# Decode block, forward and backward: Wo products of the second batch held back to row 47, and the first store tile lent by the loads for one gV only

## The chip, the cores and the metric

The kernel runs on one core of one Trainium2 chip. The metric is device time in microseconds (us), the median of several runs. The profile is of one execution.

## The reference, cut to what matters

One decode step of a pre-layernorm block with a KV cache, and the gradients of all its inputs but the constant `B_x`. There are 2 batches, 32 heads, a cache of 4096 positions and heads of 128; the model width is 640, the MLP's 1728; everything is bfloat16.

```python
q = layernorm(x) @ wq                          # [2, 32, 1, 128]
p = softmax(q @ k_cache^T * Dh**-0.5)          # per (batch, head), over 4096 positions
o = p @ v_cache
h = x + o @ wo
out = h + relu(layernorm(h) @ w1) @ w2
# and the vjp of out with grad_out:
# gV = p outer go, gK = (p * (go.V - go.o)) outer q * Dh**-0.5      [2, 32, 4096, 128] each
# go = wo @ gh, and the gradients of x, wq, wo, w1, w2
```

One (batch, head) has a K tile and a V tile of 128 x 4096 values, 1 MB each. All 64 are read, V of most heads a second time, and 64 gV and 64 gK tiles of 1 MB each are written: 211 MB read and 149 MB written in all.

## The kernel before, in words

**Rows.** The program is a hand-made plan of rows. Row i runs three steps of the forward pass for three neighbouring (batch, head) pairs: scores of pair i (K transposed by TensorE, `t_ps` into `t_sb`, then `s_ps`), the softmax and the products of K with the weights for pair i-1 (`pk`, two halves on VectorE), and the products with V for pair i-2 (`m_ps`, `u_ps`). A row has eight stages, k = 0 to 7, each ended by a `yield` in `p1_iter`. Rows 0 to 31 are the heads of batch 0 and rows 32 to 63 those of batch 1. Every 1 MB load is named here by kind and pair: K 46 is the K tile of pair 46, needed in row 46; V 43 is the V tile of pair 43, needed in row 45; W is a V tile read again for the backward pass.

**Between the stages.** After a stage of a row the loop takes, in this order: steps of the backward generator `p2_iter` (rows 41, 43, 45 and so on each begin a backward head j = 0, 1, 2; a head's steps run at k = 1 (two), 3, 4 and 6 of its own row and at k = 1, 4 and 6 of the next), at k = 5 `a_heads`, then `pump`, which issues the loads for which a tile is free, then a share of the background generators. One of these, `middle_gen(0)`, runs from row 34 on: it is the MLP of batch 0 and the gradient of its attention output, in the order layernorm, w1 products, gradient, `gh1c`, spread of `gh1c` over the partitions (`bcb_ps`), and then `go_group` for a few heads at a time (`goc`, `pr_ps`, `gom`, `d_ps`, `negdot`). Backward head j can only begin when its go is done.

**Wo products.** `a_heads(i)` does one of two things at most: `o_group`, which scales the outputs of four heads and casts them (`OU`, `OFc`, two small VectorE operations), or `a_group`, 20 TensorE products of them with Wo into `a_ps`, added to `asum` by VectorE. `a_ps` lies in the PSUM bank `mid` (bank 7), as do `pr_ps`, `d_ps` and others; the role `bc` (`bcb_ps`) takes bank 2 and bank 7 in turn in rows 34 to 40. For batch 1 the first `o_group` becomes due at row 38, and one more every four rows; `a_group` follows in the next row.

**Tiles.** Thirteen 1 MB tiles in SBUF have one of four owners, above all the loads (`ld`) and the stores (`g`). `take(tag)` hands out the tile that was given back first to that owner; `give(t, to)` gives it back, to another owner if `to` says so. A tile taken again waits, in the engine that first writes it, for all that read it before: a load waits in SyncE's queue, a gradient tile in VectorE's order waits for the landing of the store that read it. The V tiles of the last six heads of batch 0 (turns j = 0 to 5) stay in SBUF and are the W tiles of those heads, so from row 33 to row 40 seven tiles rotate among the loads. At row 40 the K tile that comes free goes to the stores (line 566). W of head 0 goes to them at row 41, W of head 2 at row 45; from then on the stores own three.

**Backward head, j < 2 (`early`).** gV is made in two VectorE halves (line 844 from 896 and 908) while W is still being transposed, and stored by GpSimd's queue (line 909); then the last score products, `gsp`, and gK in two halves (lines 938 and 940), stored at line 941. For j >= 2 gV is made after W's transposes. Loads are issued by SyncE (line 445), stores of gK and gV by GpSimd. The lines that give tiles back:

```python
        give(c["W"], "g" if j < H and j != 1 and owned["g"] < 3 else None)     # 915
        if early:
            give(gV)                                                          # 918
            yield
```

Of the kernel before, what the change touches and what calls it, by code (L numbers as in the profile page):

```python
# [15 lines left out]
def kernel(  # L16
# [23 lines left out]
    _, H, Sk, Dh = A_k_cache.shape  # L40
# [64 lines left out]
    def give(t, to=None):  # L105
        tag, k, _ = home_of.pop(id(t))
        to = to or goes_to(tag)
        owned[tag] -= 1
        owned[to] += 1
        free[to] += 1  # L110
        homes[to].append(k)
        given_at[k] = step[0]
# [736 lines left out]
    def last_dp(j, c):  # L849

        b, h = turns[j]
        pair_matvec(c["dp"], c.pop("T3"), 3, gom[:, h, b, :, :])
# [10 lines left out]
    def p2_iter(j, busy, act=0, own_gK=False, early=False):  # L863

        c = S2[j] if j < NP1 else None
        p = S2.get(j - 1)
        if p is not None:
            bp, hp = turns[j - 1]
            last_dp(j - 1, p)
            gsp = score_grad(j - 1, p)  # L870
        if c is not None:
            b, h = turns[j]
            go = gom[:, h, b, :, :]

            bank = pst([128, 512], FP32, "sps", "dp_ps")
            for k, col in enumerate((goc, qsc)):
                nc.tensor.matmul(bank[:, 128 + k * 128:256 + k * 128],  # L877
                                 lhsT=col[:, h, b:b + 1].to_broadcast([128, 128]), rhs=ident_bf[:],
                                 start=True, stop=True)
            c["dp"] = bank[:, 0:NSC]  # L880
            rb = mats.tile([128, 256], BF16, tag="rb", bufs=3, name="rb")
            nc.scalar.activation(out=rb[:], in_=bank[:, 128:384], func=ACT.Copy, scale=rt[:, b, h:h + 1])  # L882
            pp = small.tile([128, NSC, 2], BF16, tag="pp", bufs=2, name="pp")
            nc.gpsimd.tensor_copy(out=pp[:], in_=P_bf[:, b * H + h, :, None].to_broadcast([128, NSC, 2]))
            c.update(rb=rb, pp=pp)
            if act:
                pa = small.tile([128, 8], FP32, tag="pa", bufs=2, name="pa")
                nc.gpsimd.tensor_copy(out=pa[:], in_=P_bf[:, b * H + h, NSC - act:NSC])
            c["T0"] = pair_transpose(c["W"], 0, busy=busy)
        if p is not None:  # L890
            gK = take("g", [128, NSC, 128], "gK")
            outer_half(gK, p["rb"][:, 128:256], gsp, 0)
        yield
        if early:
            gV = take("g", [128, NSC, 128], "gV")
            outer_half(gV, c["rb"][:, 0:128], c["pp"], 0)
        if p is not None:
            outer_half(gK, p["rb"][:, 128:256], gsp, 1)
            nc.gpsimd.dma_start(out=natural(out_2, bp, hp), in_=gK[:])  # L899
            give(gK)  # L900
            del S2[j - 1]
        yield
        if c is None:
            return
        c["T1"] = pair_transpose(c["W"], 1, busy=busy)
        pair_matvec(c["dp"], c.pop("T0"), 0, go)
        if early:
            outer_half(gV, c["rb"][:, 0:128], c["pp"], 1)
            nc.gpsimd.dma_start(out=natural(out_3, b, h), in_=gV[:])
        yield  # L910
        c["T2"] = pair_transpose(c["W"], 2, busy=busy)
        pair_matvec(c["dp"], c.pop("T1"), 1, go)
        yield
        c["T3"] = pair_transpose(c["W"], 3, busy=busy)
        give(c["W"], "g" if j < H and j != 1 and owned["g"] < 3 else None)
        pair_matvec(c["dp"], c.pop("T2"), 2, go)
        if early:
            give(gV)
            yield
            last_dp(j, c)  # L920
            gsp = score_grad(j, c)
        else:
            gV = take("g", [128, NSC, 128], "gV")
            outer_half(gV, c["rb"][:, 0:128], c["pp"], 0)
            yield
            if own_gK:
                last_dp(j, c)
            outer_half(gV, c["rb"][:, 0:128], c["pp"], 1, act)
            for k in range(act):
                nc.scalar.activation(out=gV[:, NSC - act + k, :], in_=c["rb"][:, 0:128], func=ACT.Copy, scale=pa[:, k:k + 1])  # L930
            nc.gpsimd.dma_start(out=natural(out_3, b, h), in_=gV[:])  # L931
            give(gV)
            if own_gK:
                gsp = score_grad(j, c)
            yield
        if own_gK:
            gK = take("g", [128, NSC, 128], "gK")
            outer_half(gK, c["rb"][:, 128:256], gsp, 0)
            yield
            outer_half(gK, c["rb"][:, 128:256], gsp, 1)  # L940
            nc.gpsimd.dma_start(out=natural(out_2, b, h), in_=gK[:])
            give(gK)
            del S2[j]
            yield
# [217 lines left out]
    i = j = 0  # L1162
# [58 lines left out]
    for n, (i, j) in enumerate(plan):  # L1221
        all_go = all(("go", B - 1, h) in done for h in range(H))
        if i is None and plan[n - 1][0] is not None:
            pkp.release()
            big1 = tc.alloc_tile_pool(name="big1", bufs=1)
            for _ in range(2):
                more_home("ld", big1)
            share(ld=KEPT[1] + 4, g=5)
        if all_go and not late[0]:
            wop.release()  # L1230
            big3 = tc.alloc_tile_pool(name="big3", bufs=1, side="right")
            for tag in ("ld", "g", "g", "q", "q", "q"):
                more_home(tag, big3)
        late[0] = all_go
        more = int(late[0])
        if fin is not None and not bg2 and not bg3:
            share(ld=8 + 3 * more, g=7 + 3 * more)
        elif fin is not None and j >= H + KEPT[1] - 1:
            share(ld=5 + more, g=6 + 2 * more, f=3, q=2 + 3 * more)
        if j is not None:  # L1240
            while g2 is not None:
                p2_step()
            if j < NP1:
                bg_until(("go", *turns[j]))
            g2 = p2_iter(j, 0, 8 if i is None and j <= H else 0, i is not None and plan[n + 1][1] is None, j < EARLY)
        if i is None and ("w1", 1) in done and fin is None:
            wts.release()
            fin = tc.alloc_tile_pool(name="fin", bufs=1)
            big2 = tc.alloc_tile_pool(name="big2", bufs=1)
            more_home("f", big2)  # L1250
            banks.update(sps=[2, 3], o=[4, 5, 6])
            bg2.append(("fin", fin_gen(fin)))
            bg3.append(("gx", gx_gen(fin)))
        if i == 12:
            bg.append(("ga", ga_gen()))
        if i == H + 2:
            banks["bc"].insert(0, banks["sps"].pop(0))
        elif i == P2_AT:
            banks["bc"].remove(7)
            banks["sps"].insert(0, banks["bc"][0])  # L1260
            banks["bc"] = [7]
        rate = RATES[0 if i is not None and i <= H + 1 else 1 if j is None and i < P2_AT else
                     2 if i is not None else 3 if j <= H else 4]
        if i is None:
            spread[0] = 2
            at_k[0] = 1
            k = 0
            while g2 is not None:
                p2_step()
                pump()  # L1270
                slot[0] = int(k in ((1, 3, 5) if j <= H else (1, 4)))
                k += 1
                bg_step(0, rate)
                bg_step(1, RATE2 * (0.4 if spreading[0] else 1.0))
                bg_step(2, RATE3)
            continue
        at = MIXED if j is not None else REST
        for k, _ in enumerate(p1_iter(i, i < H + 1, 0)):
            for _ in range(at.get(k, 0)):
                if g2 is not None:  # L1280
                    p2_step()
            if k == 5:
                a_heads(i)
            pump()

            spread[0] = 1 if i < P2_AT else 2
            at_k[0] = k
            if i >= P2_AT:
                slot[0] = int(k == 6 or (k == 1 and j is not None))
            elif i > H + 1:  # L1290
                slot[0] = {1: 2, 3: 1, 4: 1, 6: 1}.get(k, 0)
            else:
                slot[0] = int(k in (1, 6))
            bg_step(0, rate)
            bg_step(1, 0.0)
        if i is not None and i in (H + 1, NP1 + 1):
            bg.append((f"m{i // H - 1}", middle_gen(i // H - 1)))
# [41 lines left out]
```

## Time and profile before

| what | value |
|---|---|
| runs shown | 889.36 us median of 3 (888.87 to 893.23) |
| the profiled execution | 888.85 us, span 886.6 us |
| busy: PE, PE weight loads, DVE, ACT, POOL | 83%, 70%, 77%, 56%, 23% |
| DMA | 361.85 MB, mean 408 GB/s |
| mean granted TensorE clock | 0.774 |
| loads of K and V: issue to landing, median | 17.3 and 18.4 us |
| stores of gV and gK: issue to landing, median | 13.6 and 14.1 us |

The page gives busy time by engine (PE is TensorE, DVE VectorE, ACT ScalarE, POOL GpSimd, SP SyncE), then the span in 40 equal slices. The mean rate of 408 GB/s stands beside slices of 410 to 427; the slices under that show where the DMA engines were not filled. Rows 35 to 52 of the plan, which the change touches, lie at about 210 to 345 us. A window's line gives its bounds, its length, the busy time and the number of instructions of each engine, the granted TensorE clock, the busy share of the DMA engines and the rate.

### The profile page before, as it was taken

How to read it: one execution, taken by the hardware profiler on the slowest of the kernel's cores; microseconds unless marked ns; L12 is line 12 of the kernel's file. 1: busy time of each engine (PE TensorE's matmuls, PEld its weight loads, DVE VectorE, ACT ScalarE, POOL GpSimd, SP SyncE). 2: the span in 40 equal slices, each digit the busy share in tenths (PEclk: the TensorE clock that was granted, in tenths of full speed). 3: DMA queues.
4: the chain of work that ended last, by engine and by line, in shares of the span. 5: the costliest groups of instructions: out<-in, count | busy, mean ns of one | idle time of the engine just before them, and what ended most of it. 6: DMA issues, size and time to landing. Idle time of an engine off the chain costs nothing.

```text
span 886.6 us, 24742 instructions
## 1 busy us (share of the span) xinstructions
PE 738.5 (83%) x10145; PEld 616.7 (70%) x10145; DVE 681.9 (77%) x1284; ACT 498.6 (56%) x1292; POOL 201.9 (23%) x358
## 2 busy tenths in 40 slices
PE   4999899899999999788868876878877898556794
PEld 4887788788888888778758766666656666345463
DVE  2666788877878897696778978878887789579964
ACT  1444343346777665455536768777656766435663
POOL 1344434443312010010012322222221111011111
PEclk9999999999999999898985555555566757556555
DMA  9999999999979999999999999999999999999997
GB/s 378 423 421 414 417 408 416 426 423 412 351 278 410 419 423 424 425 425 425 417 415 394 418 420 422 418 420 417 419 414 397 423 426 419 427 425 424 404 376 314
DMA packets 56289, 361.85 MB, mean 408 GB/s; under 512 B 5680, under 2 KB 11760, under 8 KB 15472
## 3 DMA queue, kind: packets, MB, share of 16 engines
q1 hardware_dynamic: 34520, 211.13, 57.8%
q0 software_dynamic: 18432, 134.23, 36.5%
q10 hardware_dynamic: 3224, 14.92, 4.1%
q8 instruction: 80, 1.31, 0.5%
q14 instruction: 33, 0.27, 0.1%
HBM read 211.11 MB, written 149.13 MB: 406 GB/s over the span
## 4 chain that ended last, share of the span: by engine, by line
PE 32%; DMA 31%; DVE 20%; ACT 8%; issue 7%; SPq 1%; POOL 0%; ACTq 0%; POOLq 0%; DVEq 0%
DMA Vt<-in_A_v_cache_dram 13%; PE t_ps L424 13%; PE m_ps L460 8%; DMA out_dram<-gK 7%; DVE gK L844 5%; DMA wqs<-in_A_wq_dram 5%; DVE gV L844 4%; DVE gxj L677 4%; ACT gV L930 3%; DMA out_dram<-gV 3%; PE s_ps L437 3%; DVE pk L470 3%; PE u_ps L498 2%; ACT t_sb L429 2%; PE dp_ps L437 2%
## 5 line engine op out<-in xcount | busy, mean ns | idle before, releaser
L429 ACT COPY t_sb<-t_ps 128x512 f32<-128x512 f32 x479 | 273.1, 587 | 204.5 <-PE t_ps L424 200.1
L437 PEld LDWEIGHTS <-t_sb 128*128 128x128 bf16 x4096 | 178.6, 102 | 60.8 <-ACT t_sb L429 33.6
L424 PE MATMUL t_ps<-ident_f,Wt 128*128 128x128 f32 x832 | 199.6, 391 | 0.8 <-ACT t_sb L429 0.8
L460 PE MATMUL m_ps<-pk,Vt 128*128 128x129 bf16 x2048 | 171.3, 222 | 17.1 <-DMA Vt<-in_A_v_cache_dram 16.2
L470 DVE TENSOR_TENSOR pk<-Kt,ep 128x2048 bf16<-128x2048 bf16 (+1 forms) x128 | 152.7, 1193 | 34.7 <-ACT ep L524 19.6
L844 DVE TENSOR_TENSOR gK<-rb,gsp 128x2048 bf16<-128x2048 bf16 x128 | 153.3, 1225 | 11.8 <-DMA out_dram<-gV 10.2
L424 PEld LDWEIGHTS t_ps<-ident_f,Wt 128*128 128x128 f32 x832 | 138.7, 202 | 29.9 <-issue 23.0
L460 PEld LDWEIGHTS <-Vt 128*128 128x128 bf16 x2048 | 125.1, 99 | 48.2 <-issue 28.7
L424 PE MATMUL t_ps<-ident_f,Kt 128*128 128x128 f32 x1024 | 154.3, 284 | 4.9 <-DMA Kt<-in_A_k_cache_dram 4.2
L844 DVE TENSOR_TENSOR gV<-rb,pp 128x2048 bf16<-128x2048 bf16 (+1 forms) x128 | 142.7, 1139 | 12.2 <-DMA out_dram<-gK 7.8
L486 POOL COPY pk<-ep 128x16 bf16<-128x16 bf16 x80 | 84.1, 1053 | 157.5 <-ACT ep L524 81.8
L424 PEld LDWEIGHTS t_ps<-ident_f,Kt 128*128 128x128 f32 x1024 | 112.8, 144 | 8.1 <-issue 3.3
L437 PE MATMUL dp_ps<-gom,t_sb 128*128 128x2 bf16 x2048 | 96.1, 168 | 22.5 <-ACT t_sb L429 22.3
L931 POOL DMA_DIRECT2D out_dram<-gV x62 | 33.0, 532 | 313.3 <-DVE gsp L858 116.9
L437 PE MATMUL s_ps<-qm,t_sb 128*128 128x2 bf16 x2048 | 87.3, 164 | 1.9 <-DVE t_sb L427 1.5
L986 ACT CAST ot<-o_ps 128x512 bf16<-128x512 f32 (+3 forms) x152 | 67.6, 491 | 8.0 <-DMA out_dram<-ot 3.9
L588 ACT CAST MT<-m_ps 128x128 bf16<-128x128 f32 x64 | 17.0, 266 | 91.6 <-PE m_ps L460 91.4
L899 POOL DMA_DIRECT2D out_dram<-gK x53 | 28.2, 532 | 138.5 <-DVE gK L844 104.7
L882 ACT ACTIVATE rb<-dp_ps,rt 128x256 bf16<-128x256 f32 x64 | 30.3, 473 | 46.1 <-PE dp_ps L877 45.5
L677 DVE CUSTOM_DVE_ANT_0 hbc<-wo_t,hbc 128x640 bf16<-128x640 bf16 x64 | 52.9, 826 | 0.3
L677 DVE CUSTOM_DVE_ANT_0 gxj<-wqs,gqr 128x1024 bf16<-128x1024 bf16 x40 | 48.7, 1219 | 1.2 <-DMA wqs<-in_A_wq_dram 0.9
L858 DVE SCALAR_TENSOR_TENSOR gsp<-dp_ps,negdot,P_bf 128x64 bf16<-128x64 f32 x64 | 17.9, 279 | 39.6 <-PE dp_ps L437 39.6
(205 smaller groups left out, 786.0 us busy)
## 6 DMA issues: line engine op xcount, KB each, us to landing
Kt<-in_A_k_cache_dram SPq DMA_DIRECT2D x64, 1024.0 KB, 17.3
Vt<-in_A_v_cache_dram SPq DMA_DIRECT2D x64, 1024.0 KB, 18.4
out_dram<-gV POOLq DMA_DIRECT2D x64, 1024.0 KB, 13.6
out_dram<-gK POOLq DMA_DIRECT2D x64, 1024.0 KB, 14.1
Wt<-in_A_v_cache_dram SPq DMA_DIRECT2D x52, 1024.0 KB, 11.2
wq_t<-in_A_wq_dram SPq DMA_DIRECT2D x5, 1024.0 KB, 10.0
wo_t<-in_A_wo_dram SPq DMA_DIRECT2D x4, 1280.0 KB, 18.4
wqs<-in_A_wq_dram SPq DMA_DIRECT2D x5, 1024.0 KB, 17.8
```

The lines of the kernel that those rows point to most:

```text
L424: nc.tensor.transpose(t_ps[:, j, :], natf[:, 2 * cc:2 * cc + 2, :].rearrange("p c k -> p (c k)"), ident_f[:])
L429: nc.scalar.copy(out=t_sb[:], in_=t_ps[:])
L437: nc.tensor.matmul(dst[:, sc:sc + 2], lhsT=v[:, j, :, par], rhs=vecs[:, par, :], start=(par == 0), stop=(par == 1))
L460: nc.tensor.matmul(r["m"][:, 0:129], lhsT=r["V"][:, sc, :], rhs=r["pk"][sc // HALF][:, sc % HALF, 0:129], start=(sc == 0), stop=(sc == NSC ...
L470: nc.vector.tensor_tensor(out=p["pk"][k][:, 0:n, 0:128].rearrange("p s (a two) -> p s a two", two=2), in0=p["K"][:, sl, :].rearrange("p s ...
L486: nc.gpsimd.tensor_copy(out=col, in_=e)
L677: nc.vector.tensor_tensor_reduce(out=junk[0:kc, 0:width], in0=in0, in1=in1, scale=1.0, scalar=0.0, op0=ALU.mult, op1=ALU.add, accum_out=acc)
L844: nc.vector.tensor_tensor(out=pairs_view(dst[:, sl, :]), in0=row.rearrange("p (a two) -> p a two", two=2)[:, None, :, :].to_broadcast([128 ...
L882: nc.scalar.activation(out=rb[:], in_=bank[:, 128:384], func=ACT.Copy, scale=rt[:, b, h:h + 1])
L899: nc.gpsimd.dma_start(out=natural(out_2, bp, hp), in_=gK[:])
L931: nc.gpsimd.dma_start(out=natural(out_3, b, h), in_=gV[:])
L986: nc.scalar.copy(out=ot[0:P, k, n0:n0 + nn], in_=o_ps[0:P, 0:nn])
```

## The change

```diff
         c["T3"] = pair_transpose(c["W"], 3, busy=busy)
-        give(c["W"], "g" if j < H and j != 1 and owned["g"] < 3 else None)
+        give(c["W"], "g" if j < H and owned["g"] < 3 + (j == 0) else None)
         pair_matvec(c["dp"], c.pop("T2"), 2, go)
         if early:
-            give(gV)
             yield
+            give(gV, "ld" if j == 0 else None)
             last_dp(j, c)
             gsp = score_grad(j, c)
...
-            if k == 5:
+            if k == 5 and not H + 2 < i < P2_AT + 6:
                 a_heads(i)
```

H is 32 and P2_AT is 41, so `a_heads` is not called in rows 35 to 46. The groups that were due there follow from row 47 on, one call a row. The tile of head 0's gV goes back to the loads, one stage of the plan after W's transposes (row 42, k = 1), instead of to the stores. W of head 1 goes to the stores; before, it went to the loads. From row 45 on the loads own ten tiles and the stores three, as before.

## The prediction

> **What bounds the kernel now.** I read the page's slices first, then windows of 2 us over the one hole in them, then the chain of waits there, and last the timelines of VectorE (DVE), GpSimd (POOL) and SyncE (SP).
>
> The page's slices, each 22.2 us:
>
> ```profile
> PEclk9999999999999999898985555555566757556555
> DMA  9999999999979999999999999999999999999997
> GB/s 378 423 421 414 417 408 416 426 423 412 351 278 410 419 423 424 425 425 425 417 415 394 418 420 422 418 420 417 419 414 397 423 426 419 427 425 424 404 376 314
> ```
>
> DMA sits at 410 to 427 GB/s nearly everywhere. The hole is 351 and 278, from 222 to 266 us. Outside it, time is bytes over rate, so what counts is how many microseconds of transfer a change adds or takes away. Windows over the hole's end (columns: PE, PE loads, DVE, ACT, POOL busy, PE clock, DMA share, GB/s):
>
> ```profile
> 258.00:260.00 2.00, 1.79 (x32) 1.48 (x33) 2.00 (x4) 1.71 (x6) 0.00 (x0) 1.00 0.39 160
> 260.00:262.00 2.00, 2.00 (x41) 1.60 (x34) 2.00 (x4) 0.64 (x2) 0.00 (x0) 1.00 0.03 8
> 262.00:264.00 2.00, 1.95 (x35) 1.70 (x32) 1.79 (x4) 1.11 (x5) 0.69 (x1) 1.00 0.41 172
> 264.00:266.00 2.00, 2.00 (x36) 1.98 (x36) 0.87 (x3) 1.89 (x8) 0.29 (x1) 1.00 1.08 319
> 266.00:268.00 2.00, 2.00 (x39) 1.41 (x37) 2.00 (x3) 1.48 (x4) 0.98 (x1) 1.00 0.89 340
> 268.00:270.00 2.00, 2.00 (x33) 1.86 (x30) 2.00 (x4) 1.95 (x9) 0.89 (x2) 1.00 1.01 426
> ```
>
> At 260 to 262 nothing is in flight: the loads wait for tiles, the first store has not begun, and PE and DVE are full. Row 41 begins near 255, row 42 near 263, row 43 near 269.5. Whatever shortens rows 38 to 41 brings the filled DMA forward. The chain of waits at row 39:
>
> ```profile
> 247.31 1.13 DVE pk L470
> 248.44 0.08 DVE asum L613
> 248.53 0.04 issue
> 248.57 0.44 PE bcb_ps L645 x5
> 249.01 0.88 PE t_ps L424 x8
> 249.89 0.07 PE s_ps L515
> ```
>
> PE waits for asum, because bcb_ps takes the PSUM bank that a_ps held, and asum stands in DVE's order behind a pk half.
>
> **Part one, Wo products.** Rows 35 to 46 no longer call a_heads. Gone from the hole: o_group at row 38, a_group at 39, o_group at 42, a_group at 43, o_group at 46. They come back, one a row, at rows 47 to 52 and 53 to 57; from row 58 the order is the old one.
> - Row 38, o_group: OU and OFc, 0.08 + 0.17 us, on the chain: 0.25.
> - Row 39, a_group: PE's 20 products take 0.48 of its time (chain of waits at 211.22, "0.48 PE a_ps L611 x20"), and asum holds bcb_ps. Without them bcb_ps needs gh1c, done at 247.31, so it runs 247.35 to 247.8 and t_ps to 248.7; rmax, which s_ps L515 needs, is done at 248.5. So L515 starts at 248.7 instead of 249.89: 1.15.
> - Row 42, o_group: 0.12 + 0.17 = 0.3, after the gK store but before row 43.
> The first gV store, so the refilled DMA, comes 1.4 us earlier, row 43 is entered 1.7 us earlier. The groups put back at 48, 50 and 52 cost 0.5 of PE and up to 0.8 of DVE waiting each (asum at 307.33 waits 0.80 for a_ps); there the loads of W begin (7 MB per two rows), DMA is the limit, and I cost them at nothing. If that cover is gone, three of them cost 3 x 0.8 = 2.4.
>
> **Part two, tiles.** Following take and give by hand: before, row 41's gV uses the tile lent at row 40 (call it A), W of head 0 (B) becomes a store tile, gK of head 0 uses B, and gV of head 1 uses A again. After, A goes back to the loads in row 42, so gV of head 1 must take B, and B has just been given to gK's store.
>
> ```profile
> 262.04 0.69 POOL L909 DMA_DIRECT2D out_dram<-gV  x1 [8.18 <-DVE P_bf L564]
> 269.11 0.53 POOL L941 DMA_DIRECT2D out_dram<-gK  x1 [2.13 <-DVE P_bf L564]
> ```
>
> ```profile
> 271.92 1.23 DVE L844 TENSOR_TENSOR gV<-rb,pp 128x2048 bf16<-128x2048 bf16 x1 [0.15 <-issue]
> ```
>
> That gK store (DMA to landing, its line's view over 268 to 270):
>
> ```profile
> DMA to landing us min/median/max: 7.3/7.3/7.3
> ```
>
> So it lands at 276.4, and the gV that today starts at 271.92 gets a new wait in DVE. DVE works in order: behind this gV stand gom's copies, row 43's pk halves, rmax and the second gV half; PE's d_ps waits for the gom copies (same bank), row 44's s_ps for rmax, POOL's gV store for the second half, SP's K 46 load for the pk half.
> - Load side: V 42 goes onto A, which waits in SP for gV's landing (issue 262.04, 5.3 to landing in the DMA view, less 1.4: 266); nothing behind it had a free tile before 268.6, so SP loses nothing. K 45 and V 43 follow at about 268.7; V 43 came at 277.20. One megabyte more is in flight from 266 to 277.
> - Stall: gK's store issues at 267.7 and lands 7.3 (its own row) to 9.9 us (that line's median over the kernel) later. I take 8.5, between, as it shares with one load more: 276.2. gV is wanted at 271.92 - 1.7 = 270.2: a stall of 6.0 (4.8 to 7.4).
>   "DMA: Bandwidth & Descriptors" of the Trainium skill, section Queues, rings and completion order, says that an engine takes turns between queue rows packet by packet; by that a longer load queue would not slow a store in another row, the 7.3 would hold, and the sum below would come out about 1 lower. The trace of before cannot decide it.
> - DVE afterwards: from gV's start to rmax's end it takes 6.3 us today (271.92 to 278.20); without asum and with PE ahead, 1.15 + 0.5 + 1.13 + 1.15 + 0.1 + 1.14 + 0.1 = 5.3. Row 43's rmax ends at 281.5, 3.3 late.
> - PE has two gaps of about 2.4 us, before d_ps and before row 44's s_ps. The granted clock after such gaps:
>
> ```profile
> 350.00:360.00 10.00, 8.96 (x160) 7.40 (x159) 7.73 (x14) 5.27 (x15) 0.53 (x1) 1.00 1.02 427
> 360.00:370.00 10.00, 6.16 (x69) 5.67 (x67) 3.92 (x12) 3.22 (x10) 0.78 (x2) 0.66 1.00 421
> ```
>
>   0.66 over 10 us is 6.8 us at half clock: 3.4 of work lost; 400 to 410 has 0.83, a loss of 1.7. I add 1.7 (0 to 3.4): compute is 5 us late in row 44 (2 to 8).
>   "TensorE: Matmul & The Clock Gate", Part 1, states that an idle window of about 3.4 us halves the clock; by that, gaps of 2.4 us would leave it alone and the 1.7 would be nought. The rows above show it halved in a stretch with PE 62% busy.
>
> **What DMA makes of the stall.** Issued up to 276: six tiles, 6.29 MB; moved from 262 to 276 by the 2 us windows (172, 319, 340, 426, 426, 406, 410): 5.0 MB. So 1.3 MB are in flight before the next gV store (276.25).
> - After, everything is 1.4 us earlier and fuller from 264 to 268 (about 0.25 MB), with V 43 on top: at 274.6 there are 1.3 + 1.05 - 0.25 = 2.1 MB, which at 417 GB/s last until 279.6. Lead by then: 1.4 + 0.25/0.42 = 2.0 us.
> - The gV store is issued 4.3 us after gV starts (271.92 to 276.25): 280.5; first packets 1.2 later (the first store is issued at 262.04, and the DMA view of 261 to 264 shows its bytes from 263.25): 281.7. Hole: 2.1 us (0.9 to 3.5).
> - From 284 on the same tiles are in circulation as before, only compute is 5 us late. In flight today at 284: 1.3 + 4.2 - 3.4 = 2.1 MB; at 292: 2.1 + 3.15 - 3.2 = 2.05 MB, 5 us of transfer. That just covers the lateness, without the first-packet time: 1.5 us lost (0 to 4).
> - From 317 on (W loads) DMA is oversubscribed, the lateness is absorbed, and the rest runs as now.
>
> **Sum:** -2.0 + 2.1 + 1.5 = +1.6 us on the profiled execution's 888.85 (span 886.6 and 2.25 around it): 890.5. The median shown is 0.5 above that execution, so 891.0. Ends: -2.0 + 0.9 + 0 = -1.1 (888.3) and -2.0 + 3.5 + 4 = +5.5 (894.9).
>
> **Rivals.**
> 1. The queue hides the stall whole. The extra load bridges until the late store, PE's clock holds, and only the lead remains: -1.1 to -2.5, some 887.6 on the median. For it: 2.1 MB last nearly to the new store. Against: store and loads of row 43 all come late at once. Chance 0.25.
> 2. Compute sets the pace of rows 43 to 49, so its lateness goes to the end. The waits from 262 to 300 show no engine waiting for a load: DVE and PE make those rows 15.4 us a pair, and the 2 MB in flight run out. Place: DVE at row 43's gV; price: 3.3 + 1.7 to 3.4 = 5 to 6.7, so 894.4 to 896. It decides once the lateness is over 5 us. Against: from 317 DMA wants more than it can move. Chance 0.18.
> 3. The change does not do what it says: gK's landing comes before gV is wanted, or A's return brings no earlier load; then only part one remains, 887.9. The times 276.4 and 271.92 speak against it. Chance 0.05.
> My forecast, 889.3 to 893: 0.52.
>
> **Numbers.** 0.5% is 4.4 us, about what a measurement of this kernel can tell from no change. Range 887.2 to 894.8: the forecast's own, most of rival 1, the near part of rival 2. Slower by over 0.5% (above 893.8) is rival 2 and the forecast's upper end, 0.2; faster by over 0.5% (below 884.9) would need more than the whole lead, 0.04; within, 0.76.
>
> **What would show it.** Right: in the timeline of DVE a wait of 5 to 7 us before row 43's gV, released by the gK store; V 43's load some 8 us earlier; the first gV store 1.4 us earlier, the second 4 later; a DMA hole of about 2 us near 280; halved clock near 278. Wrong: no such wait; or the DMA windows from 282 to 310 falling well under 400 GB/s, which is rival 2.

## The result, and the profile after

| kernel | median | runs | profiled execution (span) | ratio to before, 95% interval |
|---|---|---|---|---|
| before, beside it | 891.07 us (888.68 to 893.23) | 11 | 888.85 (886.6) | |
| changed | 895.23 us (893.26 to 900.07) | 11 | 894.84 (892.6) | 1.0053 (1.0038 to 1.0068) |

The change makes the kernel 0.53% slower by the ratio, 4.7 us of 891; the two medians of the table lie 4.2 apart. The forecast was +1.6 us, with a range up to 894.8. The slices of the page of the changed kernel, 22.3 us each:

```profile
DMA  9999999999988999999999999999999999999996
GB/s 379 423 419 416 415 408 418 425 423 411 352 300 325 387 423 423 425 424 425 425 376 394 417 414 419 419 415 419 415 422 406 421 425 423 424 427 425 424 417 268
```

The second slice of the old hole is a little fuller (300 for 278), and two new poor ones follow it: 325 and 387 where the kernel before had 410 and 419. They cover 268 to 312 us, rows 43 to 47. Windows of 2 us, changed kernel (columns as in the prediction):

```profile
260.00:262.00 2.00, 2.00 (x44) 1.99 (x43) 2.00 (x5) 1.00 (x3) 0.69 (x1) 1.00 0.17 70
262.00:264.00 2.00, 1.95 (x28) 1.70 (x27) 0.70 (x4) 1.94 (x7) 0.00 (x0) 1.00 1.08 356
...
278.00:280.00 2.00, 0.00 (x0) 0.00 (x0) 0.88 (x1) 0.00 (x0) 0.00 (x0) 0.96 0.98 414
280.00:282.00 2.00, 1.19 (x9) 1.19 (x10) 1.96 (x7) 0.00 (x0) 0.00 (x0) 0.50 0.39 164
282.00:284.00 2.00, 1.32 (x7) 0.92 (x5) 2.00 (x4) 1.17 (x2) 0.53 (x1) 0.50 0.05 12
284.00:286.00 2.00, 1.35 (x18) 1.35 (x19) 1.87 (x10) 0.00 (x0) 0.00 (x0) 0.50 0.78 328
286.00:288.00 2.00, 2.00 (x26) 1.94 (x27) 1.97 (x6) 1.24 (x4) 0.93 (x1) 0.50 0.99 258
```

The refill begins one window earlier (70 and 356 GB/s, where it was 8 and 172): the lead. Then DMA runs dry from 280 to 284, with all compute engines idle just before, and TensorE's (PE's) granted clock is halved (0.50). VectorE's (DVE's) timeline and the chain of waits of the changed kernel say why:

```profile
269.57 0.28 DVE L517 TENSOR_REDUCE nb<-s_ps 128x1 f32<-128x128 f32 x1
279.12 1.23 DVE L844 TENSOR_TENSOR gV<-rb,pp 128x2048 bf16<-128x2048 bf16 x1 [9.26 <-DMA out_dram<-gK]
```

```profile
267.50 11.50 DMA out_dram<-gK
279.12 0.18 DVE gV L844
```

Head 1's gV, at 271.92 before with no wait on a store, now waits 9.26 us for the landing of the gK store, which takes 11.5 us instead of 7.3. POOL's stores, SP's three loads around the first of them and one line of PE's timeline show what stands ahead of that store and what hangs on it:

```profile
267.50 0.53 POOL L941 DMA_DIRECT2D out_dram<-gK  x1 [2.13 <-DVE P_bf L564]
...
283.45 0.53 POOL L909 DMA_DIRECT2D out_dram<-gV  x1 [14.94 <-DVE P_bf L564]
```

```profile
266.31 0.33 SPq L445 DMA_DIRECT2D Vt<-in_A_v_cache_dram  x1
268.47 0.33 SPq L445 DMA_DIRECT2D Kt<-in_A_k_cache_dram  x1
268.89 0.44 SPq L445 DMA_DIRECT2D Vt<-in_A_v_cache_dram  x1
```

```profile
280.81 0.59 PE L707 MATMUL d_ps<-pr,ones_f32c 128*128 128x4 f32 x2 [4.65 <-DVE gom L345]
```

The first gV store comes 1.6 us earlier than before (260.43 for 262.04), the second 7.2 later (283.45 for 276.25), and PE stands 4.65 us behind the gom copies, which stand in DVE behind the waiting gV. The loads are V 42, issued 1.2 us ahead of the gK store, and K 45 and V 43, issued behind it.

Ten-microsecond windows, before and then changed:

```profile
270.00:280.00 10.00, 9.24 (x163) 8.34 (x163) 8.03 (x26) 5.85 (x16) 0.65 (x2) 1.00 1.01 419
280.00:290.00 10.00, 9.41 (x158) 8.31 (x159) 8.64 (x18) 8.32 (x26) 2.02 (x3) 1.00 1.01 404
290.00:300.00 10.00, 9.95 (x173) 8.54 (x165) 8.39 (x14) 5.64 (x17) 0.53 (x1) 1.00 1.01 422
300.00:310.00 10.00, 9.32 (x163) 8.26 (x162) 8.00 (x18) 6.41 (x17) 0.78 (x2) 1.00 1.01 425
310.00:320.00 10.00, 9.38 (x158) 7.96 (x155) 9.20 (x21) 6.88 (x19) 1.30 (x3) 1.00 1.01 424
```

```profile
270.00:280.00 10.00, 6.00 (x111) 5.18 (x109) 0.88 (x1) 4.36 (x13) 0.00 (x0) 0.99 1.01 391
280.00:290.00 10.00, 7.85 (x71) 6.22 (x72) 9.38 (x22) 3.63 (x10) 1.57 (x3) 0.50 0.64 237
290.00:300.00 10.00, 9.79 (x171) 9.05 (x169) 6.46 (x14) 6.76 (x20) 0.67 (x2) 1.00 1.01 411
300.00:310.00 10.00, 9.54 (x151) 8.26 (x150) 10.00 (x18) 7.58 (x22) 1.31 (x3) 1.00 1.01 384
310.00:320.00 10.00, 9.94 (x189) 8.61 (x188) 8.59 (x17) 5.39 (x15) 0.53 (x1) 1.00 1.00 389
```

The rates sum to 2094 and 1812 over five windows, so the changed kernel moves 2.82 MB less between 270 and 320 us: 6.65 us at 424 GB/s. The same subtraction is made for each experiment below and called the lost transfer time. Of the 2.82 MB, 1.67 (3.9 us) are missing from 280 to 290, where the DMA share falls to 0.64: for part of that window the engines had next to nothing to move. The other 1.15 (2.7 us) are missing from windows whose share is 1.00 or 1.01, as before: there the engines were busy and moved fewer bytes, and what slowed them is not shown. From 320 to 440 us the two kernels move 420 to 428 GB/s and nothing is won back.

### The profile page after: what moved, and what is told of

It reads as the page before. It is cut to its first block, busy times and chain, and to the rows that moved or that the text cites. A ratio compares the mean times of both kernels' runs of the same rounds, so it can differ in the third digit from the quotient of the medians.

```text
span 892.6 us, 24747 instructions
## 1 busy us (share of the span) xinstructions
PE 737.8 (83%) x10145; PEld 616.5 (69%) x10145; DVE 681.4 (76%) x1284; ACT 498.8 (56%) x1292; POOL 205.0 (23%) x358
## 4 chain that ended last, share of the span: by engine, by line
PE 38%; DMA 23%; DVE 21%; ACT 8%; issue 7%; SPq 0%; ACTq 0%; POOL 0%; POOLq 0%; DVEq 0%
PE t_ps L424 16%; DMA Vt<-in_A_v_cache_dram 11%; PE m_ps L460 9%; DVE gK L844 5%; DMA out_dram<-gK 5%; DVE gxj L677 5%; DVE gV L844 4%; DMA out_dram<-gV 3%; PE s_ps L437 3%; ACT gV L930 3%; PE u_ps L498 3%; DVE pk L470 3%; ACT t_sb L429 2%; DMA wqs<-in_A_wq_dram 2%; PE dp_ps L437 2%
## 5 line engine op out<-in xcount | busy, mean ns | idle before, releaser
L424 PE MATMUL t_ps<-ident_f,Wt 128*128 128x128 f32 x832 | 195.9, 385 | 1.1 <-ACT t_sb L429 1.1
L424 PE MATMUL t_ps<-ident_f,Kt 128*128 128x128 f32 x1024 | 157.6, 288 | 4.9 <-DMA Kt<-in_A_k_cache_dram 4.5
L424 PEld LDWEIGHTS t_ps<-ident_f,Wt 128*128 128x128 f32 x832 | 136.4, 200 | 29.6 <-issue 22.3
L424 PEld LDWEIGHTS t_ps<-ident_f,Kt 128*128 128x128 f32 x1024 | 115.1, 146 | 7.4 <-issue 3.7
L930 ACT ACTIVATE gV<-rb,pa 128x128 bf16<-128x128 bf16 x152 | 46.5, 393 | 3.3 <-DMA out_dram<-gK 3.3
## 6 DMA issues: line engine op xcount, KB each, us to landing
Wt<-in_A_v_cache_dram SPq DMA_DIRECT2D x52, 1024.0 KB, 11.5
```

Of the source, the lines that this page charges most:

```text
L424: nc.tensor.transpose(t_ps[:, j, :], natf[:, 2 * cc:2 * cc + 2, :].rearrange("p c k -> p (c k)"), ident_f[:])
```

## The experiments

The theory (A): only the wait of head 1's gV for the gK store costs, and the lost transfer goes with its length. The rivals: the Wo groups put back in rows 47 to 57 thin out the stretch after 300 us (C); the additional load does harm by itself, or the store's landing is long for another reason (B); the halved PE clock is a good part of the loss (D). The edits of e1 and e2 are shown against the kernel before, those of e3 to e8 against the changed kernel. Each ratio is to executions of the kernel before measured beside that experiment; the wait, the landing and the lost transfer are of one profiled execution each.

| kernel | wait of head 1's gV | gK store, issue to landing | lost transfer 270 to 320 | ratio to before (95%) |
|---|---|---|---|---|
| before | none on a store | 7.3 us | 0 | 1 |
| changed | 9.26 us | 11.5 | 6.65 | 1.0053 (1.0038 to 1.0068) |
| e1_wo_only | none on a store | 9.1 | 0.2 | 0.9987 (0.9973 to 1.0000) |
| e2_tiles_only | 8.80 | 11.3 | 7.7 | 1.0087 (1.0066 to 1.0107) |
| e3_stall_no_load | 7.32 | 9.6 | 6.1 | 1.0052 (1.0032 to 1.0072) |
| e4_swap | none on a store | 11.7 | 0.3 | 0.9982 (0.9966 to 0.9998) |
| e5_late_gv | none on a store | 11.8 | 0.35 | 0.9987 (0.9970 to 1.0003) |
| e6_store_first | 6.82 | 9.1 | 4.2 | 1.0040 (1.0026 to 1.0054) |
| e7_pe_busy | 9.78 | 12.0 | 5.6 | 1.0054 (1.0034 to 1.0073) |
| e8_late_same_tile | 2.60 | 11.2 | 1.8 | 0.9998 (0.9976 to 1.0019) |

**e1: the Wo edit alone.**

```diff
-            if k == 5:
+            if k == 5 and not H + 2 < i < P2_AT + 6:
```

> Only the Wo groups wait until row 47; tiles as before. Theory A (the loss is the wait of head 1's gV for the landing of the gK store): no such wait here, the first gV store at about 260.5 instead of 262.0 and the second at about 274.5 instead of 276.25, so 1.4 to 1.7 us faster than before, ratio 0.998. Rival C (the groups crowded into rows 47 to 57 slow the stretch from 304 to 314 us, where the changed kernel moves 300 to 380 GB/s): that stretch is as thin here, and the time is 1 to 2 us over before, ratio 1.001 to 1.002.

Ratio 0.9987, 1.2 us faster (0 to 2.4), and 424 and 422 GB/s in the windows from 300 to 320, where rival C wanted them thin. C falls. The profiled execution does not show the lead: its first gV store is at 262.62, and the window of 220 to 230 shows the clock at 0.83 where the profile of before has 1.00, a half-clock stretch ahead of the first group that the edit moves (242.1 before). That this stretch ate the lead is not shown. Of the eight profiled kernels with the Wo edit only the changed one, e4 and e8 have the early store (260.30 to 260.43); the other five have it at 261.87 to 263.01, and only three of these (e1, e3, e5) have the 0.83.

**e2: the tiles alone.**

```diff
-        give(c["W"], "g" if j < H and j != 1 and owned["g"] < 3 else None)
+        give(c["W"], "g" if j < H and owned["g"] < 3 + (j == 0) else None)
...
         if early:
-            give(gV)
             yield
+            give(gV, "ld" if j == 0 else None)
```

> Only the tiles change; the Wo groups stay where they were. Theory A: DVE waits 8 to 10 us before head 1's gV, the DMA engines run dry for 4 to 5 us, and without the 1.5 us lead the time is 5 to 6.5 us over before, ratio 1.006 to 1.007. Rival C: the tiles cost less than half of the loss, 2 us or under, ratio 1.002, and the stretch 25 to 35 us after the store wait is filled at 410 GB/s or more.

Ratio 1.0087: the tiles cost 7.8 us, more than the expected 5 to 6.5, and the Wo edit takes some 3 of it back. The windows after 290 are as thin as in the changed kernel (377, 385, 382) with the Wo groups in their old rows, which speaks against C once more.

**e3: the wait without the additional load.** The first store tile A goes back to the loads when W of head 1 is given up, in row 43.

```diff
+        if j == 1:
+            give(lent.pop(), "ld")
-        give(c["W"], "g" if j < H and owned["g"] < 3 + (j == 0) else None)
+        give(c["W"], "g" if j < H and owned["g"] < 4 - (j > 1) else None)
...
-            give(gV, "ld" if j == 0 else None)
+            if j == 0:
+                lent.append(gV)
+            else:
+                give(gV)
...
+    lent = []
```

> As the changed kernel, but the first store tile goes back to the loads one head later (row 43), so head 1's gV still has to take the tile of the gK store and no load comes earlier. Theory A with the load queue as the cause of the long landing (11.5 us against 7.3 before): the gK store lands in 7 to 8 us again, the wait is 5 to 6 us instead of 9.3, and it costs 2 to 4 us over before less the 1.5 lead, ratio 1.001 to 1.003. Rival B (the landing was long by chance, or for another reason than the load queued ahead of the store): landing 10 to 12, wait 9, and with 1 MB less in flight a longer hole, 6 us or more over before, ratio 1.007 or more.

DVE's timeline of this kernel:

```profile
278.83 1.23 DVE L844 TENSOR_TENSOR gV<-rb,pp 128x2048 bf16<-128x2048 bf16 x1 [7.32 <-DMA out_dram<-gK]
```

Both expectations missed half. The landing falls from 11.5 to 9.6 us and the wait from 9.26 to 7.32, in the direction of theory A though not down to its 7 to 8 and 5 to 6, but the time does not move: 1.0052. Without the additional megabyte in flight the DMA engines run dry sooner (217 GB/s from 280 to 290), so a shorter wait loses about as much. As these two profiles read, the additional load lengthens the wait by 2 us and covers about as much of it.

**e4: the lead without the wait.** A returns in row 42 as in the change, but the K tile that comes free in row 42 goes to the stores and head 1's gV takes it; W of head 1 goes to the loads as before. Wo edit in.

```diff
-            give(p["K"], "g" if i == P2_AT - 1 else None)
+            give(p["K"], "g" if i in (P2_AT - 1, P2_AT + 1) else None)
+            if i == P2_AT + 1:
+                homes["g"].insert(0, homes["g"].pop())
...
-        give(c["W"], "g" if j < H and owned["g"] < 3 + (j == 0) else None)
+        give(c["W"], "g" if j < H and j != 1 and owned["g"] < 3 else None)
```

> As the changed kernel in the Wo groups and in the return of the first store tile in row 42, but the K tile that comes free in row 42 goes to the stores and head 1's gV takes that one; W of head 1 goes to the loads as before. One load (V 42) comes some 2 us earlier, none is added, and no gV waits for a gK store. Theory A: the lead of part one stays, 1.5 to 2 us faster than before, ratio 0.998. Rival C: 1 to 2 us slower than before, ratio 1.001 to 1.002, as the groups of rows 47 to 57 are where the changed kernel has them.

```profile
270.09 1.22 DVE L846 TENSOR_TENSOR gV<-rb,pp 128x2048 bf16<-128x2048 bf16 x1 [0.34 <-ACT rb L884]
...
279.22 1.23 DVE L846 TENSOR_TENSOR gK<-rb,gsp 128x2048 bf16<-128x2048 bf16 x1 [0.85 <-DMA out_dram<-gK]
```

The gK store lands as late as in the changed kernel (11.7 us), but the first to wait for it is head 1's gK nine microseconds later, for 0.85. Ratio 0.9982, as theory A expected: the lowest of the study, though the intervals of e1 and e5 overlap its own. The transfer lost is 0.3 us.

**e5: wait gone, additional load kept.** gV of head 1 is made after W's transposes and takes the tile of that W.

```diff
-    EARLY = 2
+    EARLY = 1
...
+        if j == 1:
+            homes["g"].insert(0, homes["g"].pop())
```

> As the changed kernel, with its earlier and additional load, but head 1's gV is made after W's transposes and takes the tile of head 1's W, so it waits for no store. Theory A (only the wait costs): no wait over 1 us at that gV, no hole in the DMA windows at 280, and the lead of 1.5 to 2 us stays or the additional megabyte adds up to 1: ratio 0.997 to 0.998. Rival B (the additional load does harm by itself, by lengthening the landing of the gK store for whoever waits next): 1 us or more over before, ratio 1.001 or more.

Ratio 0.9987 (0.9970 to 1.0003), a little over theory A's 0.997 to 0.998 and under the 1.001 of rival B. V 43, issued 6 us earlier than in e1 (271.47 for 277.69), neither harms nor helps the time: e1 without it has the same ratio. In all of before, e1, e4 and e5 the DMA share is 0.95 or more from 268 on, so a megabyte more in flight there moves nothing sooner. From 270 to 280 e4 and e5 move 386 and 385 GB/s at a share of 0.99 and 1.00, as little as the changed kernel (391), so that part of its loss need not come from the wait.

**e6: the store ahead of the load.** A returns at the end of row 42, so V 42, K 45 and V 43 are all issued just behind the gK store (268.94; loads 269.92 to 271.15). Until then the tile is kept in a list, `lent`, as in e3.

```diff
-            give(gV, "ld" if j == 0 else None)
+            if j == 0:
+                lent.append(gV)
+            else:
+                give(gV)
...
             give(gK)
             del S2[j]
             yield
+            if lent:
+                give(lent.pop(), "ld")
```

> As the changed kernel, but the first store tile goes back to the loads at the end of row 42, so that the three loads of that row are issued at 268.4 to 269.5, just behind the gK store (267.5) and not one of them ahead of it. Theory A with the queue (a store's first bytes move when the loads issued before it have moved): landing 9 to 9.6 us instead of 11.5, wait 7 to 7.5 instead of 9.3, and the time 2 us under the changed kernel, ratio to before 1.003. Rival B (loads beside the store lengthen it alike, ahead or behind): landing 11 or more, ratio 1.005.

Landing 9.1 us, wait 6.82, as theory A has them. The ratio of 1.0040 lies between its 1.003 and the 1.005 of rival B, and its interval holds both, so it is the landing that tells them apart. The same three loads stand beside the store as in the changed kernel; what is different is that V 42 no longer stands ahead of it. The DMA views of the four microseconds after the issue of that store, changed kernel, then before, then e6 (queue, packets, MB, share of 16 engines; q0 carries the stores, q1 the loads):

```profile
q1 hardware_dynamic: 209, 1.47, 102.8%
```

```profile
q1 hardware_dynamic: 154, 1.03, 61.3%
q0 software_dynamic: 82, 0.67, 39.6%
```

```profile
q1 hardware_dynamic: 173, 1.16, 70.8%
q0 software_dynamic: 62, 0.51, 30.0%
```

In the changed kernel not one packet of the store moved in four microseconds, while loads went by; before, 0.67 MB of it had moved by then. Once its packets moved, loads moved beside them. The changed kernel from 273 to 274 us, then before from 272 to 273:

```profile
q0 software_dynamic: 27, 0.22, 52.1%
q1 hardware_dynamic: 25, 0.20, 48.3%
```

```profile
q0 software_dynamic: 50, 0.41, 96.7%
q1 hardware_dynamic: 1, 0.01, 1.9%
```

So the store began later and then moved more slowly. Over all ten kernels the landing is 11.2 to 12.0 where V 42 was issued ahead of the store (by 0.6 to 1.7 us) and 7.3 to 9.6 where it was not.

**e7: PE kept busy in the wait.** 24 matmuls of 512 columns ahead of the last transposes of head 1's W, overwritten by them. A second edit makes these matmuls read the same two stretches of the tile in turn.

```diff
-                             rhs=nat[:, g * GT + 4 * k:g * GT + 4 * k + 4, :].rearrange("p a b -> p (a b)"),
+                             rhs=nat[:, g * GT + 4 * (k % 2):g * GT + 4 * (k % 2) + 4, :].rearrange("p a b -> p (a b)"),
...
-        c["T3"] = pair_transpose(c["W"], 3, busy=busy)
+        c["T3"] = pair_transpose(c["W"], 3, busy=24 if j == 1 else busy)
```

> As the changed kernel, with 24 matmuls of 512 columns put ahead of the last transposes of head 1's W, whose result is overwritten; they run in the 4.65 us in which PE waits in row 43 and take 5.2 us. The granted clock then stays at 1.0 from 280 to 290. Theory A (the wait itself is what costs, and row 44 is held by DVE): within 1 us of the changed kernel, ratio to before 1.004 to 1.006. Rival D (the halved clock from 280 to 290 is a good part of the loss, as PE does 10 us of work at half speed): 3 us or more under the changed kernel, ratio 1.002 or less.

```profile
280.00:290.00 10.00, 7.58 (x98) 5.47 (x97) 8.60 (x21) 3.47 (x11) 1.46 (x2) 1.00 0.61 222
290.00:300.00 10.00, 9.21 (x158) 8.26 (x156) 7.40 (x16) 7.00 (x21) 1.08 (x2) 1.00 1.01 415
```

The clock stays at 1.00 and the ratio is 1.0054, as for the changed kernel: D falls as a good part of the loss. The windows from 300 to 320 do come back to 412 and 424 (384 and 389 in the changed kernel), so the halved clock may have a share in the thin stretch there, some 1.1 us (5.6 lost for 6.65, though with a wait of 9.78 for 9.26). The ratios do not tell it, and e3, with a clock of 0.66 from 280 to 290, has no thin stretch from 300 to 320 either (423 and 421).

**e8: the same tile, wanted 5 us later.** Only `EARLY = 1`, without the swap of e5.

> As the changed kernel, with head 1's gV made after W's transposes (some 5 us later in DVE's order) but on the same tile, that of the gK store. Wanted at about 275.5, landing at 279: a wait of 3 to 4 us instead of 9.3, with row 43's first pk half ahead of it. Theory A with a loss that goes with the wait: the wait eats the lead and a little more, ratio 0.999 to 1.002. Rival D or any fixed cost of the new order: ratio 1.004 or more.

```profile
278.64 1.23 DVE L844 TENSOR_TENSOR gV<-rb,pp 128x2048 bf16<-128x2048 bf16 x1 [2.60 <-DMA out_dram<-gK]
```

Wait 2.60 (3 to 4 expected), lost transfer 1.8, ratio 0.9998: the wait eats the lead and no more. With 0, 2.6, 6.8 and 9.3 us of wait, and the additional load in all four (e5, e8, e6, changed), the lost transfer is 0.35, 1.8, 4.2 and 6.65 us, some 0.6 to 0.7 us for each microsecond. The other two kernels with both the wait and the additional load lie to either side, e7 at 0.57 (5.6 for 9.78) and e2 at 0.88 (7.7 for 8.80). No wait, no loss; a longer wait, a larger loss: that is theory A, with a price that differs from kernel to kernel.

## Why the prediction was right or wrong, point by point

- **What bounds the kernel:** right. What DMA lost between 270 and 320 less the lead at the start is nearly what the whole kernel lost: 6.65 - 1.6 = 5.05, beside 6.0 between the two spans and 4.7 by the ratio.
- **Part one, lead of 1.4 us at the first store:** right in size as far as the times tell: 1.6 in the profile (260.43 for 262.04), 1.2 (0 to 2.4) in e1's ratio, and some 3 between the ratios of e2 and the changed kernel. Five of the eight profiles with the Wo edit do not show it, so one profile does not settle it. That the groups put back cost nothing holds (e1: 424 and 422 GB/s from 300 to 320).
- **Tiles, the new wait:** right in place, cause and order. gV of head 1 waits in DVE for the gK store, PE's d_ps stands behind gom, V 42 goes out at 266.31 (266 forecast) and V 43 at 268.89 instead of 277.20.
- **Its length: this is the step that failed.** "I take 8.5" for the gK store's landing, with 9.9 as the upper end; it took 11.5, so the wait was 9.26 instead of 6.0, outside its bounds of 4.8 to 7.4. The working counted the load in flight as sharing with the store. The runs show it ahead of the store: with V 42 issued 1.2 us before, no byte of the store moved for 4 us (e6: 9.1 with the same loads behind it). Nor was 7.3 a good lower row: the three kernels without V 42 ahead that were profiled later have 9.1 to 9.6. And the upper end was a median; the same view of before, of that line over the whole kernel, gives 11.1 as its longest landing, by which the stall would have been 8.6:

```profile
DMA to landing us min/median/max: 7.3/9.9/11.1
```

- The sentence drawn from "DMA: Bandwidth & Descriptors" of the Trainium skill, section Queues, rings and completion order, would have kept 7.3, since engines there take turns between queue rows packet by packet. The trace disagrees at the start, with no store packet in 4 us while 1.47 MB of loads went by; afterwards the two queues did move side by side (0.22 and 0.20 MB from 273 to 274). The landing was 3.0 us over the 8.5 that was taken and 4.2 over the 7.3. The trace of before hinted at it: its gK store, issued at 269.11, moved no packet before 271, while the loads in flight moved 0.4 MB a microsecond; the first gV store, with nothing in flight, began 1.2 us after its issue.
- **The DMA hole:** 2.1 us forecast. With the landing 3.0 longer the same working gives 5.1. The window from 280 to 290 lost 167 of 424 (GB/s times 10 us), 3.9 us; with the 28 lost from 270 to 280, where the engines were not idle, it is 4.6. The term was right in kind, and its size was off by its input above all.
- **The thin stretch afterwards:** 1.5 us forecast, 2.0 measured (290 to 320: 1271 for 1184). That the sizes agree is luck: the working let the transfers in flight run out, but the DMA share of those windows is 1.00 to 1.01, so the engines were busy and moved less. Why stays open. Sum with the measured terms: -1.6 + 4.6 + 2.0 = +5.0, which is 3.4 over the forecast's +1.6: 2.5 in the hole, 0.5 here and 0.4 in the lead.
- **PE's clock:** gaps forecast at 2.4 us, one was 4.65, and the clock was halved. "TensorE: Matmul & The Clock Gate", Part 1, of the Trainium skill puts the threshold at an idle window of about 3.4 us, and this gap agrees. The price that the sum's working put on the halved clock, 1.7 us of compute, is not seen in e7's ratio.
- **Rivals:** the first (the queue hides the stall) is out. The second named the right price, 5 to 6.7 us, and its sign came true, windows well under 400 from 282 to 310 (237 from 280 to 290, 384 from 300 to 310). Its reason is another one: it let compute set the pace, but from 290 on the DMA share is 1.00 or more, and after 320 the loss stays fixed because DMA is full and cannot win back what it missed. The third is out. The chance of 0.2 for over 0.5% slower and the upper end of 894.8 were too small, as the upper end of the landing was.

## What to carry to other kernels

When buffers change hands, follow by name which transfer each one was last used by, and look at the newest one first: a compute engine that works in order and takes the buffer of a store just issued waits for what is left of that store's landing (9.26 us of 11.5 here), with all that is queued behind it. Price a landing by what is issued ahead of it at that moment, not by a row with an emptier queue, and take the longest landing on record, not the median, as the upper end. Where the transfers are full afterwards, as here from 320 us on, a hole is not won back, and one load more in flight seems to have been worth something only where the DMA engines would have run dry (the changed kernel beside e3, e5 beside e1).

## What was not expected of the hardware

A store did not share with a load issued shortly ahead of it, though it goes through another queue: with 1 MB of load issued 0.6 to 1.7 us ahead it landed after 11.2 to 12.0 us in six kernels, beside 7.3 to 9.6 in the four where the same load was issued behind it. Once its packets moved, loads moved beside them (0.22 and 0.20 MB in a microsecond of the changed kernel). And the DMA engines were as busy (share 1.00 to 1.01) at 384 to 391 GB/s as at 425; the runs do not show why.
